# Tail sums divided anew between VectorE and GpSimd, tail banks exchanged, first x rows alone on one queue

## The chip, the cores and the metric

The kernel runs on one core of one Trainium2 chip. The metric is the device time of one execution in microseconds (us), the median over several runs. "Span" is the time from the first to the last instruction in the profiled run, about 2 us shorter than the device time.

## The reference

```python
def reference(A_x, A_k_cache, A_v_cache, A_wq, A_wo, B_x, B_w_gate, B_w_up, B_w_down):
    # x: 2048 rows of 640; 32 heads of 192; the window is the last 512 keys (W = Sk // 4)
    xn = _layernorm(x)
    q = (xn @ wq)                                 # to [heads, 2048, 192]
    p = softmax(einsum(q, k_last_512) * 192**-0.5)
    s = (p @ v_last_512) @ wo                     # attention, 2048 x 640
    h = _sigmoid(xn @ w_gate) * (xn @ w_up)       # 1536 wide
    g = _silu(h @ w_down)
    return x + s * g
    # (condensed by hand; all arrays are bfloat16)
```

## The kernel before

The kernel computes the gate `g` first. Then it works through 32 "units" of attention: eight groups of four heads, and in each group four blocks of 512 rows. A unit has scores (TensorE, then the exponential on ScalarE), values, and a projection with `wo` that is added over the groups into `acc`. PSUM is used as four double banks.

The last group but one (`NG - 2`) folds the gate and x into the accumulator early: GpSimd does `acc = acc * gate`, then `acc = acc + x`. The last group then needs a product and a sum for each 128 rows: `o_sb = psum * gate` on VectorE, and `out = o_sb + acc` on whichever engine `add` names. The product frees the PSUM bank; the sum frees the buffer `o_sb`, of which there are two.

```python
        nc.vector.memset(warm[:], 0.0)
        load_x(0, 1)                       # x rows 0-127   -> SP queue
        load_x(1, 1, nc.scalar)            # x rows 128-255 -> ACT queue
        load_f(nc.sync, wg_sb, wg_r, 0, 4, 0, 3)
        load_f(nc.sync, wg_sb, wg_r, 0, 4, 3, NCD)
        load_f(nc.sync, wu_sb, wu_r, 0, 4, 0, 3)
        load_x(2, 1)
        load_f(nc.sync, wu_sb, wu_r, 0, 4, 3, NCD)
        # ... cut ...

    def finish_rows(t, d0, d1, form, src, add, out_eng):
        o_sb = fin.tile([P, D], F32, name="o_sb", bufs=2)[:, d0:d1]
        r_sb = gate[:, t, d0:d1]
        nc.vector.tensor_tensor(form(o_sb), src, form(r_sb), ALU.mult)
        add.tensor_tensor(r_sb, o_sb, acc[:, t, d0:d1], ALU.add)
        out_eng.dma_start(of[t * P:(t + 1) * P, d0:d1], r_sb)

    def project(u, q, k, out_eng=None, add=nc.vector):
        # ... the matmuls, in two turns; after the first a 2-element copy "seen"
        #     orders the second turn behind it ...
        if g == NG - 1:
            finish_rows(t, 0, D, cols, res, add, out_eng)
        elif g == 0:
            nc.vector.tensor_copy(cols(acc[:, t, :]), res)
        else:
            nc.vector.tensor_tensor(cols(acc[:, t, :]), res, cols(acc[:, t, :]), ALU.add)
        if g == NG - 2:
            x_sb = fin.tile([P, D], BF16, name="row")
            nc.gpsimd.dma_start(x_sb[:], xf[t * P:(t + 1) * P, :])
            nc.gpsimd.tensor_tensor(acc[:, t, :], acc[:, t, :], gate[:, t, :], ALU.mult)
            nc.gpsimd.tensor_tensor(acc[:, t, :], acc[:, t, :], x_sb[:], ALU.add)

    order = (2, 3, 0, 1)
    # ... main loop over units 0 to 29; its last values group uses bank 0,
    #     its last projection bank 1 ...

    u = NU - 2
    passes = pairs([project(u - 2, q, 2 + q % 2, nc.sync, nc.gpsimd) for q in range(4)])
    for i in range(8):
        scores(u, *sc[i], i % 2)
        next(passes)
    passes = pairs([values(u, h, 2 + h % 2) for h in range(4)])
    for i in range(8):
        scores(u + 1, *sc[i], i % 2)
        next(passes)
    flow([values(u + 1, h, h) for h in range(4)]
         + [project(u - 1, q, q, nc.scalar, nc.gpsimd) for q in range(4)]
         + [project(u, q, q, nc.sync, nc.gpsimd if q < 3 else nc.vector) for q in range(4)])
    for q in range(4):
        last_rows(q)       # the last unit's projection, in halves of 320 columns
```

The softmax here doesn't subtract the row's maximum and nothing guards it: scores larger than these inputs give would overflow.

## Time and profile before

| | before |
|---|---|
| time (median of 3) | 931.54 us (930.91 to 932.15) |
| span of the profiled run | 929.4 us |
| TensorE busy | 917.1 us, 99% of the span |
| longest gap of TensorE | 4.86 us, at 882.5 us |
| end of the last matmul, end of the last sum, landing of the last output | 924.2, 926.8, 928.4 us |

The head of the page: the span, then busy time of each engine with its share and its number of instructions, and the first line of the chain that ended last, which is the page's guess of what the time was spent on, by engine.

```profile
span 929.4 us, 25380 instructions
PE 917.1 (99%) x11540; PEld 631.0 (68%) x11540; DVE 484.8 (52%) x978; ACT 302.2 (33%) x333; POOL 146.3 (16%) x168
...
PE 83%; DMA 6%; issue 6%; POOL 4%; DVE 1%; ACT 0%; POOLq 0%
```

TensorE is busy for 99% of the time, so nothing but fewer matmuls could win much. But the chain has DMA, "issue" and GpSimd (POOL) in it, which is odd for a kernel with a full TensorE: the last part of its time was set by something else. The timeline shows where. Its columns are start, duration, engine, line, operation, output<-inputs, shapes, count, and in brackets the idle time of the engine just before with what ended it. Other lines stand between those shown, also where no "..." marks it.

```profile
868.50 0.99 PE L489 MATMUL bank<-wo_sb,oT 64*128 64x320 bf16 x12
868.93 0.96 DVE L454 TENSOR_TENSOR o_st<-bank,rden 128x768 bf16<-128x768 f32 x1
869.95 0.82 PE L401 MATMUL bank<-qT,kT 64*128 64x512 bf16 x6 [0.45 <-DVE o_st L454]
...
881.64 0.83 PE L401 MATMUL bank<-qT,kT 64*128 64x512 bf16 x6
883.55 1.39 POOL L506 TENSOR_TENSOR acc<-acc,row 128x640 f32<-128x640 f32 x1 [0.58 <-DMA row<-in_A_x_dram]
884.90 6.01 POOL L475 TENSOR_TENSOR gate<-o_sb,acc 128x640 bf16<-128x640 f32 x4
886.46 0.82 DVE L474 TENSOR_TENSOR o_sb<-bank,gate 128x640 f32<-128x640 f32 x1 [7.36 <-POOL gate L475]
887.33 1.47 PE L441 MATMUL bank<-vbuf,E 64*128 64x193 bf16 x16 [4.86 <-DVE o_sb L474]
888.56 1.52 PE L401 MATMUL bank<-qT,kT 64*128 64x512 bf16 x6
889.84 1.31 PE L441 MATMUL bank<-vbuf,E 64*128 64x193 bf16 x16
890.98 0.83 PE L401 MATMUL bank<-qT,kT 64*128 64x512 bf16 x6
```

Read the second part from the bottom. TensorE waited 4.86 us for VectorE's product (L474), the product waited 7.36 us for GpSimd's sum (L475), and GpSimd came to its four sums only at 884.90, after its backlog of `acc + row` (L506), which itself waits for each row of x to be loaded. After the wait, three groups of matmuls last 1.47, 1.52 and 1.31 us; the same kinds of groups last 0.83 to 0.85 elsewhere (0.83 at 881.64 and 890.98). The first part is the small wait: the scores (L401) want bank 0, which VectorE is still reading (L454).

The windows view says why the groups after the stall were slow. Its columns are the window, its length, then busy time and count for PE, PEld, DVE, ACT and POOL, then the granted TensorE clock, the DMA share and GB/s.

```profile
882.00:888.00 6.00, 1.14 (x16) 0.76 (x12) 0.87 (x2) 1.09 (x2) 5.42 (x5) 0.95 0.17 55
888.00:892.00 4.00, 4.00 (x48) 2.96 (x46) 1.10 (x3) 1.18 (x2) 2.91 (x2) 0.65 0.29 101
```

The granted clock, ahead of the last two columns, is 0.65 of full speed from 888 to 892.

The end and the head of the kernel on VectorE and TensorE:

```profile
3.58 0.89 DVE L196 BATCH_NORM_STATS2 st<-x_sb 128x6 f32<-128x320 bf16 x2 [2.43 <-DMA x_sb<-in_A_x_dram]
...
16.76 1.24 PE L248 MATMUL bank<-xnT,wg_sb 128*128 128x512 bf16 x5
...
917.52 6.69 PE L516 MATMUL bank<-wo_last,oT 128*128 128x320 bf16 x48
918.59 1.42 DVE L475 TENSOR_TENSOR gate<-o_sb,acc 128x640 bf16<-128x640 f32 x1
...
926.34 0.49 DVE L475 TENSOR_TENSOR gate<-o_sb,acc 128x320 bf16<-128x320 f32 x1
```

VectorE's first statistics wait for the first rows of x until 3.58. At the end the last-rows product of TensorE (L516) is over at 924.2, and the last sum of VectorE ends at 926.83.

### The profile page before, as it was taken

Reading aid. Unit: us, or ns where it says so; the run is one execution under the profiler, and the core shown is the slowest. Engines: PE = TensorE matmul, PEld = TensorE weight load, DVE = VectorE, ACT = ScalarE, POOL = GpSimd, SP = SyncE. Lnnn points to the kernel's source line nnn. Section 1 sums busy time; section 2 is a strip of 40 time slices with the busy share of each in tenths; the row PEclk is TensorE's granted clock in tenths of the full one; section 3 lists DMA queues with packets and bytes.
Section 4 is the critical chain, followed back from the end, with each engine's and each line's share of the span. In section 5 each row is a group of like instructions: output and inputs, shape, how many; then the busy total and the mean of one; then the engine's idle time right before and its main releaser. Section 6 shows DMA issues by size and latency. Waiting matters only on the chain.

```text
span 929.4 us, 25380 instructions
## 1 busy us (share of the span) xinstructions
PE 917.1 (99%) x11540; PEld 631.0 (68%) x11540; DVE 484.8 (52%) x978; ACT 302.2 (33%) x333; POOL 146.3 (16%) x168
## 2 busy tenths in 40 slices
PE   9999999999999999999999999999999999999987
PEld 6445455465858585868686868686767676767765
DVE  5452522454646464646464646464646555555446
ACT  4222222255151515141424242424242323233330
POOL 1000100010002000200020002000200020375736
PEclk9999999999999999999999999999999999999999
DMA  9310340115435343534243354434342425253525
GB/s 315 82 29 1 88 85 1 43 63 85 87 53 113 78 67 72 109 81 72 67 107 83 65 75 101 90 55 84 90 100 46 93 90 107 51 104 100 105 55 129
DMA packets 163148, 77.15 MB, mean 83 GB/s; under 512 B 140992, under 2 KB 158608, under 8 KB 163040
## 3 DMA queue, kind: packets, MB, share of 16 engines
q1 hardware_dynamic: 155936, 53.87, 29.4%
q0 software_dynamic: 5808, 20.52, 7.7%
q8 instruction: 90, 1.47, 0.7%
q10 hardware_dynamic: 1296, 1.15, 0.4%
q14 instruction: 18, 0.15, 0.0%
HBM read 39.45 MB, written 2.62 MB: 45 GB/s over the span
## 4 chain that ended last, share of the span: by engine, by line
PE 83%; DMA 6%; issue 6%; POOL 4%; DVE 1%; ACT 0%; POOLq 0%
PE bank L419 18%; PE bank L489 17%; PE bank L441 15%; PE bank L401 15%; PE bank L248 10%; PE bank L260 6%; DMA row<-in_A_x_dram 5%; POOL acc L506 2%; PE bank L367 1%; DMA k_st<-in_A_k_cache_dram 1%; PE bank L298 1%; POOL gate L475 1%; DVE o_sb L474 0%; POOL k_perm L110 0%; POOL vbuf L118 0%
## 5 line engine op out<-in xcount | busy, mean ns | idle before, releaser
L405 ACT ACTIVATE E<-bank 128x1024 bf16<-128x1024 f32 x256 | 255.3, 1022 | 463.8 <-PE bank L401 463.7
L419 PE MATMUL bank<-xnT,wq_sb 64*128 64x512 bf16 x1800 | 226.4, 376 | 0.0
L489 PE MATMUL bank<-wo_sb,oT 64*128 64x320 bf16 x2688 | 205.2, 296 | 0.0
L401 PE MATMUL bank<-qT,kT 64*128 64x512 bf16 x1536 | 201.4, 377 | 0.4 <-DVE o_st L454 0.4
L441 PE MATMUL bank<-vbuf,E 64*128 64x193 bf16 x4096 | 196.4, 244 | 4.9 <-DVE o_sb L474 4.9
L441 PEld LDWEIGHTS <-E 64*128 64x128 bf16 x4096 | 179.8, 94 | 15.5 <-issue 6.0
L489 PEld LDWEIGHTS <-oT 64*128 64x128 bf16 x2976 | 164.6, 94 | 29.2
L426 DVE CAST qT<-bank 128x1024 bf16<-128x1024 f32 x90 | 110.2, 1224 | 128.5 <-PE bank L419 128.5
L419 PEld LDWEIGHTS <-wq_sb 64*128 64x128 bf16 x1800 | 105.9, 100 | 87.2 <-issue 0.4
L401 PEld LDWEIGHTS <-kT 64*128 64x128 bf16 x1536 | 88.3, 94 | 74.3 <-issue 0.9
L454 DVE TENSOR_TENSOR o_st<-bank,rden 128x768 bf16<-128x768 f32 x128 | 122.5, 957 | 4.4
L501 DVE TENSOR_TENSOR acc<-bank,acc 128x640 f32<-128x640 f32 x96 | 79.0, 823 | 20.3 <-PE bank L489 20.3
L118 POOL DMA_DIRECT2D vbuf<-in_A_v_cache_dram x28 | 21.1, 753 | 312.8 <-PE bank L441 309.9
L424 DVE COPY seen<-bank 128x2 f32<-128x2 f32 x90 | 14.3, 159 | 79.1 <-PE bank L419 79.1
L453 DVE RECIPROCAL rden<-bank 128x4 f32<-128x4 f32 x128 | 23.3, 182 | 60.6 <-PE bank L441 59.6
L248 PE MATMUL bank<-xnT,wg_sb 128*128 128x512 bf16 x220 | 54.7, 379 | 0.0
L248 PE MATMUL bank<-xnT,wu_sb 128*128 128x512 bf16 x220 | 54.7, 379 | 0.0
L260 PE MATMUL bank<-wd_sb,hT 128*128 128x512 bf16 (+1 forms) x384 | 52.8, 299 | 0.0
L254 DVE TENSOR_TENSOR hT<-bank,sig 128x512 bf16<-128x512 f32 x44 | 30.3, 689 | 42.7 <-ACT sig L251 42.7
L251 ACT ACTIVATE sig<-bank 128x512 bf16<-128x512 f32 x44 | 26.3, 597 | 68.4 <-PE bank L248 65.3
L260 PEld LDWEIGHTS <-hT 128*128 128x128 bf16 x384 | 29.7, 98 | 23.1
L97 POOL DMA_DIRECT2D wq_sb<-in_A_wq_dram x7 | 6.3, 900 | 210.6 <-PE bank L419 210.6
(55 smaller groups left out, 387.0 us busy)
## 6 DMA issues: line engine op xcount, KB each, us to landing
wo_sb<-in_A_wo_dram SPq DMA_DIRECT2D x7, 960.0 KB, 5.5
wq_sb<-in_A_wq_dram POOLq DMA_DIRECT2D x7, 960.0 KB, 5.8
k_st<-in_A_k_cache_dram POOLq DMA_DIRECT2D x14, 384.0 KB, 5.4
vbuf<-in_A_v_cache_dram POOLq DMA_DIRECT2D x28, 192.0 KB, 3.3
row<-in_A_x_dram POOLq DMA_DIRECT2D x16, 160.0 KB, 2.7
oT<-o_st SPq DMA_TRANSPOSE x128, 3.4
x_sb<-in_A_x_dram SPq DMA_DIRECT2D x3, 640.0 KB, 10.2
wd_sb<-in_B_w_down_dram SPq DMA_DIRECT2D x1, 1920.0 KB, 13.9
```

The lines of the kernel that those rows point to most:

```text
L248: nc.tensor.matmul(bank[k][:, half, 0:r1 - r0], lhsT=w[:, c, f * P:(f + 1) * P], rhs=xnT[:, b, c, r0:r1], start=(c == 0), stop=(c == NCD - 1))
L251: nc.scalar.activation(sig[:, 0:r1 - r0], bank[k][:, 0, 0:r1 - r0], AF.Sigmoid)
L254: nc.vector.tensor_tensor(hT[b][:, f, r0:r1], bank[k][:, 1, 0:r1 - r0], sig[:, 0:r1 - r0], ALU.mult)
L260: nc.tensor.matmul(wide(k)[:, d0:d1], lhsT=hT[b][:, f, q * P:(q + 1) * P], rhs=wd_sb[:, f, d0:d1], start=(f == 0), stop=(f == NF - 1))
L401: nc.tensor.matmul(bank[k][:, i, :], lhsT=kT[r, pr, j, c * P:(c + 1) * P], rhs=q[r, pr * DJ + j, :], start=(j == 0), stop=(j == DJ - 1))
L405: nc.scalar.activation(E[u, pr][:, c, :, :], bank[k][:], AF.Exp, scale=scale_qk)
L419: nc.tensor.matmul(bank[k][:, half, :], lhsT=wq[r, c, col:col + DJ * (P - 1) + 1:DJ], rhs=xnT[r, b, c, :], start=(c == 0 and not second), ...
L426: nc.vector.tensor_copy(qT[u][:, 2 * m:2 * m + 2, :], bank[k][:])
L441: nc.tensor.matmul(o4[:, q, 0:DH + 1], lhsT=e[r, c, h % 2, q * P:(q + 1) * P], rhs=vbuf[r, h, c, 0:DH + 1], start=(turn == 0 and qq == 0 a ...
L454: nc.vector.tensor_tensor(o_st[u][:, :, h * DH:(h + 1) * DH], o4[:, :, 0:DH], rden[:].to_broadcast([P, TQ, DH]), ALU.mult)
L489: nc.tensor.matmul(res[:, half, :], lhsT=oT[u][r, cc, q * P:(q + 1) * P], rhs=wo[r, cc, half * HD:(half + 1) * HD], start=(turn == 0 and c ...
L501: nc.vector.tensor_tensor(cols(acc[:, t, :]), res, cols(acc[:, t, :]), ALU.add)
```

## The change

The intent: take GpSimd's late sums out of the path, let VectorE put each last sum behind the next product, so that banks are freed sooner, let the tail's first scores find free banks, and let the first rows of x arrive alone.

```diff
-        def load_x(t, n, eng=nc.sync):
+        def load_x(t, n):
 ...
+        nc.vector.memset(wg_sb[:, 0, 0:2], 0.0)
         load_x(0, 1)
-        load_x(1, 1, nc.scalar)
-        load_f(nc.sync, wg_sb, wg_r, 0, 4, 0, 3)
+        load_x(1, 1)
+        load_f(nc.scalar, wg_sb, wg_r, 0, 4, 0, 3)
 ... (finish_rows is split into gated_rows, the product, and stored_rows, the sum and the store)
-    def last_rows(q):
-        ... k = (2 * q + i) % 4 ...
-            finish_rows(..., nc.gpsimd if 2 * q + i < 5 else nc.vector, ...)
+    def last_rows():
+        wait = []
+        for q in range(TQ):
+            o = fin.tile([P, D], F32, name="o_sb", bufs=2)
+            for i in range(2):
+                k = order[(2 * q + i) % 4]
+                ... matmuls ...
+                gated_rows(o, t, d0, d1, bank[k][:, 0, 0:HD])
+                args = (o, t, d0, d1, nc.gpsimd if q < 2 else nc.vector, ...)
+                if q < 2:
+                    stored_rows(*args)
+                    continue
+                wait.append(args)
+                while len(wait) > (1 if (q, i) < (3, 0) else 0):
+                    stored_rows(*wait.pop(0))
 ...
-    passes = pairs([project(u - 2, q, 2 + q % 2, nc.sync, nc.gpsimd) for q in range(4)])
+    passes = pairs([project(u - 2, q, q % 2, nc.sync) for q in range(4)])
     for i in range(8):
-        scores(u, *sc[i], i % 2)
+        scores(u, *sc[i], 2 + i % 2)
 ...
-    passes = pairs([values(u, h, 2 + h % 2) for h in range(4)])
+    passes = pairs([values(u, h, h % 2) for h in range(4)])
-        scores(u + 1, *sc[i], i % 2)
+        scores(u + 1, *sc[i], 2 + i % 2)
 ... (values, project and last_rows behind them: bank q becomes bank order[q])
-         + [project(u, q, q, nc.sync, nc.gpsimd if q < 3 else nc.vector) for q in range(4)])
+         + [project(u, q, order[q], nc.sync, nc.gpsimd if q < 2 else nc.vector) for q in range(4)])
```

The memset of two elements of `wg_sb` makes the weights' load, now on the ACT queue, wait for VectorE, so that it goes out 0.45 us behind the first rows of x.

Some words for what follows. The "head" is the start of the kernel, up to the first gate matmuls that are 512 wide (the "first full gated group"); the "tail" is what comes after the main loop. x0 and x1 are the first two tiles of 128 rows of x. The unit that the texts call the third-last is unit 28 (`u - 2` with `u = 30`), the fourth-last of units 0 to 31.

More of the change, by code (lines that the diff above doesn't have):

```diff
@@ L153 @@
         xt = {}
-        def load_x(t, n, eng=nc.sync):
+        def load_x(t, n):
             x = xpool.tile([P, n, D], BF16, name=f"x_sb{n}", bufs=4 if n == 1 else 2)
-            eng.dma_start(x[:], xf[t * P:(t + n) * P, :].rearrange("(q p) d -> p q d", p=P))
+            nc.sync.dma_start(x[:], xf[t * P:(t + n) * P, :].rearrange("(q p) d -> p q d", p=P))
             for i in range(n):
@@ L468, in cols, with gated_rows, stored_rows @@
         return x.rearrange("p (i n) -> p i n", i=2)
-    def finish_rows(t, d0, d1, form, src, add, out_eng):
-        o_sb = fin.tile([P, D], F32, name="o_sb", bufs=2)[:, d0:d1]
+    def gated_rows(o, t, d0, d1, src, form=lambda x: x):
+        nc.vector.tensor_tensor(form(o[:, d0:d1]), src, form(gate[:, t, d0:d1]), ALU.mult)
+    def stored_rows(o, t, d0, d1, add, out_eng):
         r_sb = gate[:, t, d0:d1]
-        nc.vector.tensor_tensor(form(o_sb), src, form(r_sb), ALU.mult)
-        add.tensor_tensor(r_sb, o_sb, acc[:, t, d0:d1], ALU.add)
+        add.tensor_tensor(r_sb, o[:, d0:d1], acc[:, t, d0:d1], ALU.add)
         out_eng.dma_start(of[t * P:(t + 1) * P, d0:d1], r_sb)
@@ L496, in project @@
         if g == NG - 1:
-            finish_rows(t, 0, D, cols, res, add, out_eng)
+            o = fin.tile([P, D], F32, name="o_sb", bufs=2)
+            gated_rows(o, t, 0, D, res, cols)
+            stored_rows(o, t, 0, D, add, out_eng)
         elif g == 0:
@@ L507, in project @@
         yield
-    def last_rows(q):
-        u = NU - 1
-        t = (NB - 1) * TQ + q
-        for i in range(2):
-            k = (2 * q + i) % 4
-            for cc in range(GC):
-                nc.tensor.matmul(bank[k][:, 0, 0:HD], lhsT=oT[u][:, cc, q * P:(q + 1) * P],
-                                 rhs=grp[NG - 1]["wo"][:, cc, i * HD:(i + 1) * HD],
-                                 start=(cc == 0), stop=(cc == GC - 1))
-            finish_rows(t, i * HD, (i + 1) * HD, lambda x: x, bank[k][:, 0, 0:HD],
-                        nc.gpsimd if 2 * q + i < 5 else nc.vector, (nc.scalar, nc.sync)[i])
+    def last_rows():
+        wait = []
+        for q in range(TQ):
+            t = (NB - 1) * TQ + q
+            o = fin.tile([P, D], F32, name="o_sb", bufs=2)
+            for i in range(2):
+                d0, d1 = i * HD, (i + 1) * HD
+                k = order[(2 * q + i) % 4]
+                for cc in range(GC):
+                    nc.tensor.matmul(bank[k][:, 0, 0:HD],
+                                     lhsT=oT[NU - 1][:, cc, q * P:(q + 1) * P],
+                                     rhs=grp[NG - 1]["wo"][:, cc, d0:d1],
+                                     start=(cc == 0), stop=(cc == GC - 1))
+                gated_rows(o, t, d0, d1, bank[k][:, 0, 0:HD])
+                args = (o, t, d0, d1, nc.gpsimd if q < 2 else nc.vector, (nc.scalar, nc.sync)[i])
+                if q < 2:
[4 more added lines that the diff above has]
+                    stored_rows(*wait.pop(0))
     def flow(jobs):
@@ L575 @@
     u = NU - 2
-    passes = pairs([project(u - 2, q, 2 + q % 2, nc.sync, nc.gpsimd) for q in range(4)])
+    passes = pairs([project(u - 2, q, q % 2, nc.sync) for q in range(4)])
     for i in range(8):
-        scores(u, *sc[i], i % 2)
+        scores(u, *sc[i], 2 + i % 2)
         next(passes)
-    passes = pairs([values(u, h, 2 + h % 2) for h in range(4)])
+    passes = pairs([values(u, h, h % 2) for h in range(4)])
     for i in range(8):
-        scores(u + 1, *sc[i], i % 2)
+        scores(u + 1, *sc[i], 2 + i % 2)
         next(passes)
-    flow([values(u + 1, h, h) for h in range(4)]
-         + [project(u - 1, q, q, nc.scalar, nc.gpsimd) for q in range(4)]
-         + [project(u, q, q, nc.sync, nc.gpsimd if q < 3 else nc.vector) for q in range(4)])
-    for q in range(4):
-        last_rows(q)
+    flow([values(u + 1, h, order[h]) for h in range(4)]
+         + [project(u - 1, q, order[q], nc.scalar, nc.gpsimd) for q in range(4)]
+         + [project(u, q, order[q], nc.sync, nc.gpsimd if q < 2 else nc.vector) for q in range(4)])
+    last_rows()
 _INS = ['A_x', 'A_k_cache', 'A_v_cache', 'A_wq', 'A_wo', 'B_x', 'B_w_gate', 'B_w_up', 'B_w_down']
```

## The prediction

> **What bounds it.** TensorE: the page gives PE 917.1 us busy of a 929.4 us span (99%), clock 0.998. The timeline shows three places where time can be had without removing matmuls.
>
> 1. *A stall, 882.5 to 887.3.* TensorE waits 4.86 us for VectorE's product o_sb, which waits 7.36 us for GpSimd's sum (gate<-o_sb,acc). That sum stands behind GpSimd's backlog of acc*gate and acc+row (1.4 us each, the last ends at 884.9), and o_sb has two buffers. The windows view then shows granted clock 0.65 for 888 to 892: the first three groups after the stall (values, scores, values) take 3.65 us (887.33 to 890.98); at the later pace of 1.31 us per scores+values pair they would take 1.97. So the stall costs 4.86 + 1.7 = 6.5 us. That idling lowers the clock is what the Trainium skill says (TensorE: Matmul & The Clock Gate, Part 1); the 0.65 agrees.
> 2. *A bank wait at 869.5:* 0.45 us, until o_st has been read from bank 0.
> 3. *Ends:* the last matmul ends at 924.2, the last sum at 926.83. At the head, statistics start at 3.58, x rows land at 3.55 and 3.78.
>
> **What the change does.**
> - The third-last unit's four sums move to VectorE. Their acc rows were finished long before (the program waits for earlier GpSimd updates only), so the backlog leaves the path: -6.5 us. Cost: four sums of 0.82 us (estimate: the 320-wide sum takes 0.49, the 640-wide product 0.82) where VectorE is busy 3.9 of 13 us. But they have two SBUF inputs; by the Trainium skill (SBUF — State Buffer, "Who interferes with whom") such an operation and a GpSimd operation reading SBUF exclude each other. The trace agrees: the one 640-wide VectorE sum, at 918.59, took 1.42 us and ended 0.68 after GpSimd's sum at 919.33. Each may wait up to 1.4 us. Stepping through by hand, the "seen" copies behind them still come 0.5 us before TensorE needs them: no new stall.
> - Exchanged banks: scores go to 2 and 3, free at 869; projections use 0 and 1 one group later: -0.45 us.
> - Tail: six projections' sums stay on GpSimd (1.54 us each, paced by TensorE at 1.63), two go to VectorE; last rows: four halves each, each VectorE sum behind the next product. VectorE still lags 1.6 us behind the last matmul: it does 12 operations of 0.5 us and waits for buffers and port: -0.25 us.
> - Head: x0 alone lands 0.3 us earlier (packets of both x tiles overlapped from 2.0 to 3.1). But the up-weights' second piece landed at 8.65, its matmuls began at 8.71; x2 landed at 7.94, used at 7.96: later loads bind. -0.15 us.
>
> Sum -7.3 us: **924.3 us**, range 923.0 to 926.5; 0.8%, so within 2%: 0.98; faster 0.015; slower 0.005.
>
> **Signs.** No TensorE gap above 0.5 us between 865 and 900, clock 1.00 there; 1.31 us per pair from the first on; VectorE sums between 874 and 884 of 0.8 to 2.2 us, several stretched by GpSimd; the end after the last matmul still about 5 us; first weight matmuls at 6.1 rather than 6.4, tile 1's at most 0.2 earlier.
>
> **What would make it wrong.** The exclusion delaying VectorE so that "seen" copies hold TensorE (1 to 3 us less gain); the tail's VectorE sums blocked behind GpSimd (end 0.5 later); weights on the second queue landing late.

## The result

The changed kernel takes 923.21 us (median of 4, 922.92 to 923.81) against 931.22 us for the kernel before in the same rounds. The ratio is 0.9914, 95% interval 0.9896 to 0.9931. (A ratio is the mean time of one kernel's fast runs over that of the other's of the same rounds, so not quite the ratio of the quoted medians.) That is 8.0 us; 7.2 us were forecast (931.5 to 924.3). A second measurement, as one of the experiments, gave 923.45 us and 0.9913 (0.9898 to 0.9928).

The page's head and the chain after:

```profile
span 921.2 us, 25377 instructions
PE 915.1 (99%) x11540; PEld 630.2 (68%) x11540; DVE 489.8 (53%) x985; ACT 302.3 (33%) x333; POOL 138.2 (15%) x162
...
PE 99%; DMA 1%; SPq 0%; DVE 0%; issue 0%
```

DMA, "issue" and GpSimd have all but gone from the chain, which is now 99% TensorE. The lines that answer to those shown of before (PE L492 is the projection, L403 the scores, L443 the values; DVE L473 the product, L478 the sum):

```profile
868.02 0.99 PE L492 MATMUL bank<-wo_sb,oT 64*128 64x320 bf16 x12
...
868.84 0.83 PE L403 MATMUL bank<-qT,kT 64*128 64x512 bf16 x6
...
874.37 0.83 DVE L478 TENSOR_TENSOR gate<-o_sb,acc 128x640 bf16<-128x640 f32 x1
874.83 1.62 POOL L511 TENSOR_TENSOR acc<-acc,row 128x640 f32<-128x640 f32 x1 [1.02 <-DMA row<-in_A_x_dram]
876.03 1.10 DVE L478 TENSOR_TENSOR gate<-o_sb,acc 128x640 bf16<-128x640 f32 x1
...
880.54 0.83 PE L403 MATMUL bank<-qT,kT 64*128 64x512 bf16 x6
881.09 1.39 POOL L511 TENSOR_TENSOR acc<-acc,row 128x640 f32<-128x640 f32 x1 [2.68 <-DMA row<-in_A_x_dram]
881.18 0.84 PE L443 MATMUL bank<-vbuf,E 64*128 64x193 bf16 x16
...
881.88 1.28 DVE L478 TENSOR_TENSOR gate<-o_sb,acc 128x640 bf16<-128x640 f32 x1
...
883.16 0.83 PE L403 MATMUL bank<-qT,kT 64*128 64x512 bf16 x6
```

No bracket stands behind a TensorE line any more: both waits are gone. Three groups after 881.18 take 1.98 us instead of 3.65. The sums on VectorE take 0.83 us, or 1.10 and 1.28 us where a GpSimd operation was under way (876.03 + 1.10 = 877.13, 0.68 us after the end of GpSimd's operation, 874.83 + 1.62 = 876.45; likewise 883.16 and 882.48), and GpSimd's own at 874.83 took 1.62 instead of 1.39 us, as it had to wait for VectorE. GpSimd's backlog ends no sooner than before (its last `acc + row` at 886.56, against 884.93); nothing waits for it.

```profile
882.00:888.00 6.00, 6.00 (x102) 4.54 (x98) 3.74 (x8) 4.61 (x6) 3.81 (x4) 1.00 0.26 82
888.00:892.00 4.00, 4.00 (x83) 3.38 (x80) 2.00 (x5) 3.04 (x3) 0.00 (x0) 1.00 0.00 0
```

The granted clock is 1.00 in both windows. The head and the end:

```profile
3.14 0.89 DVE L198 BATCH_NORM_STATS2 st<-x_sb 128x6 f32<-128x320 bf16 x2 [1.99 <-DMA x_sb<-in_A_x_dram]
...
16.27 1.24 PE L250 MATMUL bank<-xnT,wg_sb 128*128 128x512 bf16 x5
...
909.71 6.69 PE L525 MATMUL bank<-wo_last,oT 128*128 128x320 bf16 x48
912.26 1.68 DVE L473 TENSOR_TENSOR o_sb<-bank,gate 128x320 f32<-128x320 f32 x4
...
915.35 1.15 DVE L478 TENSOR_TENSOR gate<-o_sb,acc 128x320 bf16<-128x320 f32 x1
...
918.13 0.49 DVE L478 TENSOR_TENSOR gate<-o_sb,acc 128x320 bf16<-128x320 f32 x1
```

The starts of TensorE's groups cut both traces into the same pieces, and the pieces add up to the whole difference of 8.2 us:

| piece | before | after | gain | forecast |
|---|---|---|---|---|
| start to the first full gated group (L248 / L250) | 16.76 | 16.27 | 0.49 | 0.15 |
| from there to the main loop's last projection (868.50 / 868.02) | 851.74 | 851.75 | 0 | 0 |
| last projection to the first tail scores | 1.45 | 0.82 | 0.63 | 0.45 |
| those scores to the first values group (the stall) | 17.38 | 12.34 | 5.04 | 4.86 |
| values group to the first last-rows product (the slow clock) | 30.19 | 28.53 | 1.66 | 1.7 |
| first last-rows product to the end of the last sum | 9.31 | 8.92 | 0.39 | 0.25 |
| last sum to the end of the span | 2.57 | 2.58 | 0 | 0 |

### The profile page after: what moved, and what is told of

It reads as the page before. It is cut to its first block, busy times and chain, and to the rows that moved or that the text cites. A ratio compares the mean times of both kernels' runs of the same rounds, so it can differ in the third digit from the quotient of the medians.

```text
span 921.2 us, 25377 instructions
## 1 busy us (share of the span) xinstructions
PE 915.1 (99%) x11540; PEld 630.2 (68%) x11540; DVE 489.8 (53%) x985; ACT 302.3 (33%) x333; POOL 138.2 (15%) x162
## 4 chain that ended last, share of the span: by engine, by line
PE 99%; DMA 1%; SPq 0%; DVE 0%; issue 0%
PE bank L492 22%; PE bank L421 21%; PE bank L443 19%; PE bank L403 18%; PE bank L250 10%; PE bank L262 6%; PE bank L369 1%; PE bank L300 1%; PE bank L525 1%; DMA wu_sb<-in_B_w_up_dram 1%; SPq L158 0%; DVE gate L478 0%; SPq L163 0%; DVE o_sb L473 0%; PE bank L230 0%
## 5 line engine op out<-in xcount | busy, mean ns | idle before, releaser
L492 PE MATMUL bank<-wo_sb,oT 64*128 64x320 bf16 x2688 | 205.2, 296 | 0.0
L403 PE MATMUL bank<-qT,kT 64*128 64x512 bf16 x1536 | 200.8, 376 | 0.0
L443 PE MATMUL bank<-vbuf,E 64*128 64x193 bf16 x4096 | 195.4, 243 | 0.0
L443 PEld LDWEIGHTS <-E 64*128 64x128 bf16 x4096 | 178.9, 94 | 10.1 <-issue 0.3
L492 PEld LDWEIGHTS <-oT 64*128 64x128 bf16 x2976 | 164.8, 94 | 29.1
L403 PEld LDWEIGHTS <-kT 64*128 64x128 bf16 x1536 | 88.2, 94 | 73.4
L250 PE MATMUL bank<-xnT,wu_sb 128*128 128x512 bf16 x220 | 54.7, 379 | 0.0
L250 PE MATMUL bank<-xnT,wg_sb 128*128 128x512 bf16 x220 | 54.7, 379 | 0.0
L256 DVE TENSOR_TENSOR hT<-bank,sig 128x512 bf16<-128x512 f32 x44 | 30.3, 689 | 42.0 <-ACT sig L253 42.0
L250 PEld LDWEIGHTS <-wu_sb 128*128 128x128 bf16 x220 | 21.5, 98 | 26.0
```

The lines of the kernel that those rows point to most:

```text
L250: nc.tensor.matmul(bank[k][:, half, 0:r1 - r0], lhsT=w[:, c, f * P:(f + 1) * P], rhs=xnT[:, b, c, r0:r1], start=(c == 0), stop=(c == NCD - 1))
L256: nc.vector.tensor_tensor(hT[b][:, f, r0:r1], bank[k][:, 1, 0:r1 - r0], sig[:, 0:r1 - r0], ALU.mult)
L403: nc.tensor.matmul(bank[k][:, i, :], lhsT=kT[r, pr, j, c * P:(c + 1) * P], rhs=q[r, pr * DJ + j, :], start=(j == 0), stop=(j == DJ - 1))
L443: nc.tensor.matmul(o4[:, q, 0:DH + 1], lhsT=e[r, c, h % 2, q * P:(q + 1) * P], rhs=vbuf[r, h, c, 0:DH + 1], start=(turn == 0 and qq == 0 a ...
L492: nc.tensor.matmul(res[:, half, :], lhsT=oT[u][r, cc, q * P:(q + 1) * P], rhs=wo[r, cc, half * HD:(half + 1) * HD], start=(turn == 0 and c ...
```

## The experiments

Twelve kernels ran (e1 to e4, e5 to e8, e9 to e12), each on one chip with its own runs of the kernel before. All gave correct results. Effects of half a microsecond are hard to see in the times: the kernel before alone scatters from 928.4 to 933.4 us. So the pieces of the trace are given too:

| kernel | scores to values | values to last rows | last rows to last sum |
|---|---|---|---|
| before | 17.38 | 30.19 | 9.31 |
| changed | 12.34 | 28.53 | 8.92 |
| e1 sums alone | 12.35 | 28.52 | 9.33 |
| e2 four buffers | 12.34 | 28.53 | 9.31 |
| e3 clock kept | 16.88 | 28.52 | 9.32 |
| e4 banks alone | 19.07 | 30.32 | 9.32 |
| e5 changed, old banks | 12.66 | 29.01 | 8.92 |
| e6 head alone | 17.28 | 31.10 | 9.32 |
| e7 changed, weights not held back | 12.35 | 28.52 | 8.92 |
| e8 tail alone | 17.18 | 31.07 | 8.92 |
| e9 more on VectorE at the end | 12.34 | 28.72 | 9.01 |
| e10 changed, old head | 12.35 | 28.64 | 8.93 |
| e11 changed, again | 12.35 | 28.53 | 8.92 |
| e12 changed, head on one queue | 12.35 | 28.53 | 8.92 |

### e1: only the four sums moved

```diff
 (before)
-    passes = pairs([project(u - 2, q, 2 + q % 2, nc.sync, nc.gpsimd) for q in range(4)])
+    passes = pairs([project(u - 2, q, 2 + q % 2, nc.sync) for q in range(4)])
```

> Before, with only the third-last unit's four sums moved from GpSimd to VectorE. My theory (the sum stands behind GpSimd's backlog, VectorE's product waits for its buffer, TensorE for the bank): the 4.9 us gap of TensorE at 882 is gone and so is the slow clock after it, -6.5 us (924.5 to 925.1); the four VectorE sums take 0.8 to 1.3 us. Rival (the gain of the change comes mostly from the exchanged banks and the tail, and the stall only moves to another wait when the sums are moved alone): less than 4 us of gain and a new TensorE gap near 880.

Measured: 925.06 us against 930.81, ratio 0.9941 (0.9928 to 0.9954). The stall and the slow clock are both gone from the trace, and no new gap appears; the four sums took 0.82, 1.10, 0.82 and 1.10 us. This one argument of the diff is worth 5.8 us by the medians, 6.7 us by the pieces of the two traces (5.03 + 1.67). The expectation of 924.5 to 925.1 holds, but the gain by the medians is 0.7 us under the 6.5 forecast: in the other runs of the kernel before, the stall and its slow clock need not cost what they cost in the one trace (see e8). The rival falls.

### e2: the sums left on GpSimd, but four buffers

```diff
 (before, in project)
+            more = None
+            if u == NU - 4 and q >= 2:
+                if q == 2:
+                    grp["o"] = load1.tile([P, 2, GW], F32, name="o_more", tag="k_perm")
+                more = grp["o"][:, q - 2, 0:D]
-            finish_rows(t, 0, D, cols, res, add, out_eng)
+            finish_rows(t, 0, D, cols, res, add, out_eng, more)   # more: used as o_sb
```

The third and fourth product went into a key tile that is dead by then.

> Before, with the sums left on GpSimd, but four buffers for the products of the third-last unit (two of them in the memory of the dead key tile), so that no product waits for a sum. If it is the buffer wait alone that carries GpSimd's lateness to TensorE: the 4.9 us gap goes as in e1, -6.5 us, with GpSimd's sums still ending near 891. If GpSimd's lateness reaches TensorE in another way (through the port, through the acc rows), a gap of over 1 us stays and the gain is under 5 us.

Measured: 924.93 us, ratio 0.9939 (0.9925 to 0.9954), 0.13 us from e1. The trace has TensorE run on while GpSimd is as late as ever:

```profile
883.06 0.85 PE L441 MATMUL bank<-vbuf,E 64*128 64x193 bf16 x16
883.87 3.04 POOL L476 TENSOR_TENSOR gate<-o_sb,acc 128x640 bf16<-128x640 f32 x2
...
886.87 3.03 POOL L476 TENSOR_TENSOR gate<-o_more,acc 128x640 bf16<-128x640 f32 x2
```

GpSimd's sums end at 889.9, seven us after TensorE began the values. So the lateness of GpSimd did no harm in itself; it reached TensorE only through the two buffers. Moving the work or giving it room are equally good cures.

### e3: the stall kept, TensorE kept busy in it

```diff
 (before)
     for i in range(8):
         scores(u + 1, *sc[i], i % 2)
+        if i == 0:
+            for _ in range(20):
+                nc.tensor.matmul(bank[1][:, 1, :], lhsT=warm[:, 0:P], rhs=warm[:],
+                                 start=True, stop=True)
         next(passes)
```

> Before, with the stall left in and 20 useless 512-wide products on a free bank issued by TensorE at its start (0.216 us each at full clock, 4.3 us of 4.9). Theory (the groups after the stall are slow because the clock dropped while TensorE idled): the granted clock stays at 1.00 from 887 to 892, values-scores-values after the stall take about 2.0 us instead of 3.65, time -1.7 us (929.5), the stall itself stays. Rival (those groups are slow because VectorE and GpSimd are behind, or because instruction fetch starts anew): the three groups still take over 3 us and the time stays within 0.5 us of before.

Measured: 929.76 us against 930.81, ratio 0.9994 (0.9981 to 1.0007): the times leave the gain open (the profiled run starts its first full gated group 0.99 us later than the run of before, at 17.75, which the edit does not touch). The trace does not:

```profile
883.40 4.49 PE L585 MATMUL bank<-warm 128*128 128x512 bf16 x19
887.83 0.84 PE L441 MATMUL bank<-vbuf,E 64*128 64x193 bf16 x16
...
889.82 0.81 PE L401 MATMUL bank<-qT,kT 64*128 64x512 bf16 x6
```

The stall is still there, filled with useless products (the record of one of the 20 is missing), and the three groups after it take 1.99 us instead of 3.65, at a granted clock of 1.00. From the values to the last rows it takes 28.52 us, what the kernel without a stall takes. VectorE and GpSimd are just as late as before, so their lateness is not what made the groups slow: it is TensorE's own idling. The stall of 4.9 us thus cost its own length and, in this pair of traces, another 1.7 us.

### e4: only the banks exchanged

```diff
 (before; likewise for all banks of the tail)
-    passes = pairs([project(u - 2, q, 2 + q % 2, nc.sync, nc.gpsimd) for q in range(4)])
+    passes = pairs([project(u - 2, q, q % 2, nc.sync, nc.gpsimd) for q in range(4)])
-        scores(u, *sc[i], i % 2)
+        scores(u, *sc[i], 2 + i % 2)
```

> Before, with only the banks exchanged from the second-last unit on. The 0.45 us TensorE gap at 869.5 goes. Theory: the stall at 882 ends when GpSimd's backlog ends, which the banks do not touch, so the 0.5 us is eaten by a longer stall: time within 0.2 us of before and the stall some 0.5 to 0.6 us longer (about 5.4). Rival (the gains are independent and add up): -0.5 to -0.6 us, stall unchanged at 4.86.

Measured: 931.82 us (926.88 to 933.32) against 930.81, ratio 1.0008 (0.9988 to 1.0028). The wait before the scores is gone (they start at 869.31), and the stall takes it back:

```profile
888.38 1.48 PE L441 MATMUL bank<-vbuf,E 64*128 64x193 bf16 x16 [6.54 <-DVE o_sb L474]
```

The stall is 6.54 us. Of the 1.68 us more than before, 0.64 are the scores' earlier start; the rest is GpSimd, whose last row sum ended 1.05 us later in this run (885.98 against 884.93). The stall ends when GpSimd's backlog ends, whatever TensorE does before it, so the exchange alone wins nothing. The rival, that gains add up, falls for this one. The sizes were missed: 5.4 us were expected for the stall, and a time within 0.2 us of before where the medians differ by 1.0. GpSimd's backlog does not end at the same time in every run; the brackets show its sums waiting for the loads of x rows, but that those loads cause the scatter was not tested.

### e5: the changed kernel with the old banks

```diff
 (changed; likewise for all banks of the tail)
-    passes = pairs([project(u - 2, q, q % 2, nc.sync) for q in range(4)])
+    passes = pairs([project(u - 2, q, 2 + q % 2, nc.sync) for q in range(4)])
```

> The changed kernel with the old banks. If the exchange is worth what the traces say once the stall is gone: a TensorE gap of about 0.45 us before the second-last unit's scores and 0.5 to 0.65 us more than the changed kernel (923.7 to 923.9 against 923.2). If the exchange is worth nothing: within 0.2 us of it and no gap.

Measured: 924.06 us (923.69 to 926.40), ratio 0.9935 (0.9920 to 0.9949). The gap of 0.45 us before the scores is back, and from the last projection to the scores it takes 0.63 us more again. So the exchange is worth that, once the stall is gone; every trace with the old banks has 1.44 or 1.45 us there, every one with the new banks 0.81 or 0.82. The times say less: 924.06 is a little over the expected 923.7 to 923.9. The profiled run happened to be the slowest. Most of that is the head (its first full gated group starts at 18.27, 2.00 us later than in the changed kernel; see e10 to e12), but it shows something else too:

```profile
882.93 1.41 POOL L510 TENSOR_TENSOR acc<-acc,gate 128x640 f32<-128x640 f32 x1
883.16 1.88 DVE L478 TENSOR_TENSOR gate<-o_sb,acc 128x640 bf16<-128x640 f32 x1
884.96 0.81 DVE L473 TENSOR_TENSOR o_sb<-bank,gate 128x640 f32<-128x640 f32 x1
885.83 0.84 PE L443 MATMUL bank<-vbuf,E 64*128 64x193 bf16 x16 [0.21 <-DVE o_sb L473]
```

Here VectorE was ready for two of its sums just after GpSimd had started an operation, waited it out, and took 1.96 (at 876.99, not shown) and 1.88 us. The product behind the second one came late enough to hold TensorE by 0.21 us; the columns of the table show 0.32 and 0.48 us lost. That is the failure that the prediction feared, at a small scale. It goes with the moment at which GpSimd starts relative to VectorE, and not with the banks: e1 has the old banks and loses nothing, while e9 and e10, with the new banks, have first sums of 1.41 and 1.48 us and lose 0.2 and 0.1 us between values and last rows.

### e6: only the head changed

```diff
 (before)
+        nc.vector.memset(wg_sb[:, 0, 0:2], 0.0)
         load_x(0, 1)
-        load_x(1, 1, nc.scalar)
-        load_f(nc.sync, wg_sb, wg_r, 0, 4, 0, 3)
+        load_x(1, 1)
+        load_f(nc.scalar, wg_sb, wg_r, 0, 4, 0, 3)
```

> Before, with only the head of the change (x tiles one after the other on one queue, first gate weights on the other queue behind a small memset). I forecast 0.15 us for it; the two traces show that from the first full gated group on (16.76 against 16.27) 0.49 us is won. If the head alone does that: same landing times as after (x0 near 3.1, second piece of the up-weights near 8.45), first full gated group near 16.27, -0.5 us. If it was run-to-run scatter of the loads: 16.5 to 16.8 and under 0.25 us.

Measured: 931.53 us against 931.11, ratio 1.0013 (0.9995 to 1.0031). No gain in time. In the trace, x0 lands at 3.00, the first full gated group starts at 16.35 (0.41 us earlier than before), and the lead of 0.41 us still stands at the tail's scores. It is then lost: the slow clock after the stall cost 0.9 us more (31.10 us from values to last rows, against 30.19).

### e7: the changed kernel without holding the weights back

```diff
 (changed)
-        nc.vector.memset(wg_sb[:, 0, 0:2], 0.0)
```

> The changed kernel without the memset that holds the weights back, so that the weights' load goes out at 0.74 beside x0. Theory (x0 lands early because its packets have the engines alone): x0 lands near 3.5 again, first statistics at 3.5 and the whole head some 0.3 to 0.45 us later than the changed kernel. Rival (it is the second queue, or fewer issues on the first, that wins): x0 lands at 3.1 to 3.2 and the head stays as in the changed kernel or gets better, as the weights land earlier.

Measured: 924.32 us (923.87 to 925.71), ratio 0.9936 (0.9923 to 0.9949). x0 lands at 3.40 instead of 3.12, nearly as late as before (3.55), so in this one trace the theory holds for x0: it is early because its packets have the engines alone. But x1 lands at 4.98, and the first full gated group starts only at 18.26, 2.0 us later than in the changed kernel where 0.3 to 0.45 were expected. The size was missed; e10 to e12 say what the rest is.

### e8: only the tail's sums divided anew

```diff
 (before; last_rows, gated_rows and stored_rows as in the change, with the old banks)
-         + [project(u, q, q, nc.sync, nc.gpsimd if q < 3 else nc.vector) for q in range(4)])
-    for q in range(4):
-        last_rows(q)
+         + [project(u, q, q, nc.sync, nc.gpsimd if q < 2 else nc.vector) for q in range(4)])
+    last_rows()
```

> Before, with only the tail's sums divided anew (and each last sum behind the next product). The stall at 882 stays, with the slow clock. From the first last-rows product of TensorE to the end of the last sum: 9.31 us before, 8.85 in the changed kernel; if the tail alone does that, -0.4 to -0.5 us. If the tail's gain came from the other parts, 9.2 or more and no gain.

Measured: 932.87 us against 931.11, ratio 1.0020 (1.0003 to 1.0037): not faster, if anything slower. The trace shows the expected 0.39 us at the end (8.92 against 9.31) and, as in e6, 0.9 us more lost to the slow clock; the windows of e8 show a granted clock of 0.50 from 888 to 892, where before had 0.65.

```profile
882.00:888.00 6.00, 1.35 (x17) 1.03 (x15) 1.15 (x2) 1.03 (x2) 5.34 (x5) 0.79 0.14 48
888.00:892.00 4.00, 4.00 (x36) 2.66 (x32) 0.82 (x3) 1.02 (x1) 2.63 (x2) 0.50 0.35 122
892.00:896.00 4.00, 4.00 (x68) 2.98 (x66) 2.44 (x5) 2.92 (x3) 0.00 (x0) 0.96 0.02 5
```

How long the clock stays low after the stall differs between traces (28.5 us from values to last rows without a drop; 30.2, 30.3, 31.1 and 31.1 with one). The windows show by how much: before's mean clock of 0.95 over 6 us and 0.65 over 4 us makes 3.4 us at half speed, e8's 0.79, 0.50 and 0.96 make 6.8 us, twice as long. The clock record of the traces has the edges: 0.50 from 887.39 to 890.80 in the kernel before, and from 885.28 to 892.10 in e4, 885.32 to 892.14 in e6 and 885.48 to 892.31 in e8.

Only the part behind the stall costs time, and half of it: by this estimate 1.7 us in before, 1.9 in e4, 2.7 in e6 and 2.6 in e8, where the table shows 1.66, 1.79, 2.57 and 2.54. The slow stretch does not come in every run: one run of e4 had a mean granted clock of 1.000 and took 926.88 us, its five others had 0.996 or 0.997 and took 930.5 to 933.3. Why before got the short stretch and e6 and e8 the long one stays open; it does not matter for the changed kernel, which has no stall.

### e9: more of the end on VectorE

```diff
 (changed)
-         + [project(u - 1, q, order[q], nc.scalar, nc.gpsimd) for q in range(4)]
-         + [project(u, q, order[q], nc.sync, nc.gpsimd if q < 2 else nc.vector) for q in range(4)])
+         + [project(u - 1, q, order[q], nc.scalar, nc.vector if q == 2 else nc.gpsimd) for q in range(4)]
+         + [project(u, q, order[q], nc.sync, nc.gpsimd if q % 2 else nc.vector) for q in range(4)])
 (and in last_rows all sums on nc.vector, each behind the next product, four buffers)
```

> A version that should beat the changed kernel: all eight last-rows sums on VectorE, three of the eight earlier tail sums on VectorE (where it has slack) and the last of them on GpSimd, and two more buffers for the last products. Theory (VectorE is the limit after the last product, and waits for GpSimd's port and buffers cost it 1.7 us there): no VectorE sum of the last rows over 0.6 us, and from the first last-rows product of TensorE to the last sum 8.0 us instead of 8.92: about -0.9 us against the changed kernel run beside it. Rival (the port makes the two engines' sums exclude each other anyway, so moving them only moves the wait): 8.7 us or more.

Measured: 923.46 us against 923.45 for the unchanged copy beside it. No gain, and 9.01 us from the first last-rows product to the last sum, against 8.92 (8.0 were expected, and no sum over 0.6 us). The theory had the right engine and the wrong part of its time:

```profile
912.60 1.26 DVE L478 TENSOR_TENSOR gate<-o_sb,acc 128x320 bf16<-128x320 f32 x1
913.78 0.48 DVE L473 TENSOR_TENSOR o_sb<-bank,gate 128x320 f32<-128x320 f32 x1
914.18 0.48 DVE L478 TENSOR_TENSOR gate<-o_sb,acc 128x320 bf16<-128x320 f32 x1
...
918.70 0.49 DVE L478 TENSOR_TENSOR gate<-o_more,acc 128x320 bf16<-128x320 f32 x1
```

One sum waits for GpSimd (1.26 us); from then on VectorE hardly waits, starting an operation every 0.40 us. But it has 13 of them to do from 913.78 on, and ends no sooner. The waits in the changed kernel's end are real, but giving GpSimd a part of the sums spares VectorE about as much as the waits cost: the two ends come out within 0.1 us.

### e10, e11, e12: the head by itself

e10 is the changed kernel with the old head (the diff of e6 backwards), e11 the changed kernel unchanged, e12 the changed kernel with x0, x1 and the first weights all on the SP queue:

```diff
 (changed, e12)
-        nc.vector.memset(wg_sb[:, 0, 0:2], 0.0)
         load_x(0, 1)
         load_x(1, 1)
-        load_f(nc.scalar, wg_sb, wg_r, 0, 4, 0, 3)
+        load_f(nc.sync, wg_sb, wg_r, 0, 4, 0, 3)
```

> The changed kernel with the old head, to be compared with the unchanged copy in the same rounds; without the stall, nothing after the head can swallow or add to its gain. If the head is worth 0.5 us as the first two traces say: 0.4 to 0.6 us slower than the copy. If that was scatter (the first full gated group began between 16.3 and 18.3 in the ten traces so far, with either head): within 0.3 us of the copy. x0 should land near 3.55 and x1 near 3.75.

> The changed kernel unchanged, beside the three others. 923.2 as on record, within 0.6. The head's start of the first full gated group is the open number: 16.3 if the trace on record was typical, up to 18.3 if x1 lands late (3.9 to 5.0 in the four traces with this head, as it shares the engines with the first weights).

> The changed kernel with its head on one queue: x0, x1, then the first gate weights, no second queue and no memset. Theory (x1's scatter comes from sharing the engines with the weights on the other queue): x0 near 3.1, x1 at 3.4 to 3.7 and steady, first full gated group at 16.3 or earlier, 0.2 to 1.0 us faster than the copy on average. Rival (the second queue speeds the weights up, and that is worth more): first gate weights land 0.3 or more later than 5.2 to 5.8, and no gain.

Measured in the same rounds: e10 923.67 us (923.47 to 923.98), e11 923.45 (923.23 to 923.63), e12 923.50 (923.21 to 924.73). The old head costs 0.22 us by the medians, with overlapping ranges. What the traces say of the loads:

| head | traces | x0 lands | x1 lands | first full gated group |
|---|---|---|---|---|
| old | 7 | 3.52 to 3.88 | 3.56 to 3.85 | 16.69 to 17.75, median 16.82 |
| changed | 5 | 3.00 to 3.15 | 3.83 to 4.94 | 16.27 to 18.27, median 16.53 |
| changed, weights not held back (e7) | 1 | 3.40 | 4.98 | 18.26 |
| one queue (e12) | 1 | 2.93 | 3.54 | 16.67 |

The changed head brings x0 earlier in every trace (medians 3.57 and 3.13), and x1 later in all but one, where it lands within the old head's range. The two cases with x1 after 4.9, e5 and e7, are the two that start the gated groups past 18.2. Their first gate group starts 0.73 and 0.77 us later than in the changed kernel; the other 1.2 us are slow matmuls: that group's 20 products take 2.32 and 2.33 us instead of 1.28, and matmuls start 107 ns apart instead of 56 until 9.59 and 9.53. Twice the time is what a clock of 0.50 would give, so that is the likely cause (the clock record begins later and cannot show it). Whether x1's lateness causes it was not tested; TensorE idles 0.78 and 0.82 us just before in these two. e12 does make x1 early, but all weights behind it land later (the first gate weights at 5.85 instead of 5.2 to 5.8, the first up-weights at 7.67 instead of 7.0 to 7.6, and their matmuls start at 7.71), and its time is that of e11: nothing is gained. The 0.49 us of the first pair of traces was partly luck of the loads.

No version beats the changed kernel by more than the scatter.

## Why the prediction was right

The forecast was 924.3 us with a range of 923.0 to 926.5, and 923.2 was measured. Point by point:

1. *The stall: -6.5 us forecast, 6.70 in the traces (5.04 + 1.66).* Right, in mechanism too. e1 shows that the four sums are the cause, e2 that the two buffers carry it, e3 that the second part is the clock. That the 1.7 us fit to 0.04 is partly luck: they were read off the trace of before with which they are compared here, and other traces with the stall lose 1.79 to 2.57. The 4.86 us read from the bracket were 0.18 too few, because a bracket counts from the modelled end of the group before, and matmul groups normally start some 0.17 us before that end (after: the projection at 868.02 lasts 0.99 us, the scores start at 868.84). To price a wait, compare starts with starts.
2. *The banks: -0.45 forecast, 0.63 measured.* The same error of 0.18 us. The prediction took it for an independent gain; e4 shows that it is worth nothing while the stall is there, e5 that it is worth its 0.6 us when the stall is gone.
3. *The tail: -0.25 forecast, 0.39 measured*, in every trace with the new tail, to within 0.02 us except for e9. The prediction said that VectorE would still lag, and it does: its last sum ends 2.2 us after the last matmul, against 2.6 before (the 1.6 us of the forecast is what before's trace shows up to the start of the last product, 925.82 against 924.21; after the change it is 1.2).
4. *The head: -0.15 forecast, 0.49 in the first pair of traces, 0.22 in the times of e10 and e11.* The step that failed is "later loads bind". The later loads landed 0.2 us earlier themselves (second piece of the up-weights at 8.45 instead of 8.65), and the wait for them was absorbed by idle time that tile 1's group had before it: that group started at 9.02 instead of 9.50, where "at most 0.2 earlier" was forecast. On average over more runs the size forecast was nearer than the first trace.
5. *The exclusion of VectorE's and GpSimd's reads.* Forecast as sums of 0.8 to 2.2 us without a new stall. On record they were 0.83 to 1.28 us; over the runs up to 1.96 us, and once they cost TensorE (e5). The fear was right in kind, and the margin of 0.5 us on the "seen" copies was thin but mostly enough.

The sum was 0.7 to 0.9 us short, 0.18 twice from reading brackets, 0.14 from the tail and the rest from the head.

That the gains add up at all is owed to the stall's being gone. The Trainium skill (TensorE: Matmul & The Clock Gate, Part 1) says that TensorE's clock drops after an idle window of about 3.4 us and comes back after as long a busy one, by a free-running window; the traces agree in the length of the slow stretches (3.41 us at a granted clock of 0.50 in before, 6.83 us in e4, e6 and e8; the drop came 3.1 to 4.9 us into the stall), and e3 shows the consequence, 1.66 us. The Trainium skill (SBUF — State Buffer, "Who interferes with whom") says that a VectorE operation with two SBUF inputs and a GpSimd operation that reads SBUF exclude each other. The stretched 640-wide sums agree: in the changed kernel they end 0.68 us after the GpSimd operation that stood in their way, which is most of the 0.83 us that a sum takes alone.

## What to carry to other kernels

A slow helper engine hurts through the buffers it holds: before moving its work, ask which buffer or bank the critical engine waits for, and note that one or two more buffers may do as well (e1 and e2 are 0.13 us apart). A long stall can swallow a gain ahead of it (e4), and the varying slow clock behind it can hide one (e6, e8), so remove it first and judge small changes afterwards. A long stall of TensorE can cost more than its idle time, and a gain of half a microsecond at the head should be measured over several runs, not read from one pair of traces.

## What the Trainium skill lacked or had wrong

- TensorE: Matmul & The Clock Gate, Part 1, works out the penalty of a kernel that stalls in every turn of its loop as half of the time at the low clock, but gives no price for a single stall. Here stalls of 4.65 to 6.54 us cost a further 1.7 to 2.6 us (28.5 us from values to last rows without the drop, 30.2 to 31.1 with it), which is half of the low-clock time that falls behind the stall; useless products in the stall took that to zero.
- SBUF — State Buffer, "Who interferes with whom", has the exclusion right, but no number for two tensor_tensor operations that alternate. Here a VectorE sum of 0.83 us became 1.10 to 1.96 us, according to how long before it GpSimd had started, and a GpSimd operation of 1.39 us became 1.51 to 1.98.
- VectorE: DVE Perf Modes, Terms, says that the next operation cannot issue until the pipeline has emptied; the page's own section on the DRAIN limits this to operations that are held. In the records, independent 320-wide operations of 0.48 us start every 0.40 us (e9), so the records of neighbours overlap by 0.08 us; a dependent one starts 0.04 us after the end (918.70 in e9, after a product that ended at 918.66).
- Trainium Kernel Development and Optimization, Key Constraints, says that transfers from all queues share the same DMA engines and interleave. The runs agree, and add what it does to a small load: x1 landed at 3.54 us with one queue (one trace) and between 3.83 and 4.94 with the weights on a second queue (five traces). No page has the scatter of the first loads from run to run.
